# Block-sorted attention into a gated layer on one core: value products, a key-sort group and an exponential in another order within two down layers

## The chip, the cores and the metric

The kernel runs on one core of one Trainium2 chip. The metric is the device time of one execution in microseconds; lower is better. The inputs are 4 batches of 8 heads with 768 tokens of 64 values, and the weights of a gated layer of width 2048 on 512 features.

## The reference

Attention with sorted blocks, whose output goes through a gated layer. Per batch and head an 8x8 matrix `P` (five rounds of exponential and normalisation of `sort_net`) mixes the 8 blocks of 96 keys and of 96 values; each block of 96 queries attends to the mixed block in its place:

```python
k_sorted = np.einsum('bhij,bhjcd->bhicd', P, k_b).reshape(B, H, S, D)
v_sorted = np.einsum('bhij,bhjcd->bhicd', P, v_b).reshape(B, H, S, D)
...
scores = scale * np.matmul(q_b, k_sb.transpose(0, 1, 2, 4, 3))
scores = scores - np.max(scores, axis=-1, keepdims=True)
attn = np.exp(scores)
attn = attn / (np.sum(attn, axis=-1, keepdims=True) + 1e-09)
return np.matmul(attn, v_sb).reshape(B, H, S, D).astype(np.float32)
...
h = x @ w_in
g = h * np.cos(h)
return (g @ w_out).astype(np.float32)
```

## The kernel before

**Chunks and blocks.** The 3072 tokens are worked off in 8 chunks `n` of 384 tokens (half a batch), each of 4 blocks `u` of 96 queries. "Block (3,1)" is block 1 of chunk 3. A chunk goes through attention, then an up layer (`moe_up`) and a down layer (`moe_down`). The order of all instructions is written out by hand, engine by engine: each engine does its own in the order in which the code calls them. The attention of chunk n+1 (and the first scores of chunk n+2) stands between the matmuls of chunk n's layers.

**Attention of a block**, by name of the step:

- scores `sc`: 8 groups of matmuls of the block's queries (`q_turned`) on sorted keys (`kTs`), on TensorE (PE), by `by_half` (L504) or `scores` (L438);
- maximum `mx` (L489) and subtraction `s` (L491) on VectorE (DVE);
- `expo`: the exponential into `p_buf` on ScalarE (ACT, L570). Then `p_buf` is transposed into `pT`, by a DMA that SP issues (L588), or, with `True` as its last argument, later by PE (`p_transpose`). The `pT` of blocks (3,0) and (4,0) lies in a part of the buffer `kv`;
- `av`: the value product, 8 matmuls of 96x65 elements (L625) on sorted values `vS`; column 65 gives the sum. DVE normalises it into `xn` (L636, L638). `xn` is transposed into `xT` by a DMA of SP (L644), or, with `True`, by PE (`x_transpose`, L656, with a copy on DVE).

**Layers.** `up` is 8 matmuls of 384 columns into `h` (L669), a cosine on ACT (L673) and a product on DVE (L677); a chunk has 8 of them and they read all of its `xT`. `down(n, ts, half)` is 8 matmuls of 512 columns into `o` (L694) for 128 tokens; a chunk has three token tiles `ts` of two halves each. In `moe_down` these six are the steps e = 0 to 5: what stands in `slots[e]` comes behind step e, what stands in `mid[e]` between its fourth and fifth matmul. Behind a tile's second half its `o` is copied (ACT, or DVE for the last) and stored by SP (L684).

**Sorting.** The keys and values of the second pair of batches are sorted in groups: `k_sort_g` (4 matmuls `ks`, L408, and a cast on ACT into `kTs`, L257), and `batch`, which does several groups in a row: scores by `by_half`, keys (`ks`) or values (`vs`) by `sort_eight` (16 matmuls, L518, and a cast on ACT). When all keys are sorted, `k_swap(kT2)` moves two thirds of them to the other half of the partitions with two DMAs of SP (L421, L422); chunks 4 to 7 read the result.

**Buffers.** PSUM has 3 buffers of the pool `big` (scores, sort groups, value products, `h`) and 2 of `acc` (`o` and a few others). A tile takes the buffer that was given out longest ago and waits until its last reader is done.

**Queues.** SP issues, in this order, around the change: the transposes of chunk 3's queries (L149, two), of `pT` (2,0), (2,1), (2,2), two stores, `pT` (3,0), a store, the transposes of chunk 4's queries (L149, two), `k_swap` (L421, L422), `pT` (3,1), (3,2), a store, `pT` (3,3), `xT` (3,0), `xT` (3,1), a store. GpSimd (POOL) loads queries and values (L129, L92). Before chunk 4's queries it holds (`p_hold`, L596) until the `pT` of (2,2) has landed, and before chunk 5's until that of (3,3) has.

The change is in two places: chunk 1's down layer, written out at L1130 to L1154 of the kernel below, and the table of chunk 2's at L1162 to L1167.

Of the kernel before, what the change touches and what calls it, by code (L numbers as in the profile page):

```python
# [18 lines left out]
def kernel(  # L19
# [15 lines left out]
    nc = tc.nc  # L35
    B, H, S, D = q.shape
# [110 lines left out]
    def q_transpose_dma(n):  # L147
        for e in range(2):
            nc.sync.dma_start_transpose(  # L149
                out=q_of(n, e)[:, :QW].rearrange("p (x c) -> p x c", c=blk),  # L150
                in_=q_zeroed(n)[:, e * QZ:(e + 1) * QZ])
# [101 lines left out]
    V, A = nc.vector, nc.scalar  # L253

    def copy_on(eng, dst, src):
        if eng is nc.scalar:
            eng.copy(dst, src)  # L257
        else:
            eng.tensor_copy(dst, src)  # L259
# [147 lines left out]
    def k_products(ps, t, c, rows, rhs, keys=kbuf):  # L407
        nc.tensor.matmul(  # L408
            ps[:, t], keys[rows, c * 2 * D:(c + 1) * 2 * D], rhs, start=True, stop=True)

    def k_sort_g(t0, eng, pool, tag):
        ps = pool.tile([128, 4, 4 * NB], FP32, name="ks", tag=tag)
        for t in range(4):
            k_products(ps, t, t0 + t, slice(0, 128), bds[1].rearrange("p x i -> p (x i)"),
                       pair)
        copy_on(
            eng, kT2[:, ::2, :, :, t0:t0 + 4].rearrange("p e b m t -> p b e m t"),
            ps.rearrange("p t (b e m) -> p b e m t", b=2, e=2))
# [114 lines left out]
    def batch(*parts, between=()):  # L533

        tiles = []
        for kind, *x in parts:
            ps = big.tile([128, 2, 512], FP32, name=kind, tag="big")
            tiles.append(ps)
            if kind == "sc":
                by_half(*x, ps)  # L540
            else:
                sort_eight(kind, x[0], ps)
        step(between)
        for (kind, *x), ps in zip(parts, tiles):
            if kind == "sc":
                s_t[tuple(x)] = sp.tile([blk, 2, H2, blk], FP32, name="s", tag="s")
                qk_reduce(*x, [0, 1], ps)
            else:
                place_eight(kind, *x[:1], ps, x[1])
# [60 lines left out]
    def av(n, u, on_pe=False):  # L610
        av_products(n, u)
        av_norm(n, u, on_pe)

    def av_products(n, u, fill=0):
        g, b2, ih = where(n)
        if n not in xT:
            xT[n] = xtp.tile([128, KC, TC], BF16, name="xT", tag="xT")
        a = big.tile([128, 2, 512], FP32, name="av", tag="big")
        keep_warm(fill, a[:, 0], 256)
        pt = pT.pop((n, u)).rearrange("p a c -> p (a c)")  # L620
        for hp in range(2):
            for h2 in range(H2):
                e = hp * H2 + h2
                w = 128 if e < 2 * H2 - 1 else blk
                nc.tensor.matmul(  # L625
                    a[:w, hp, h2 * (D + 1):(h2 + 1) * (D + 1)],
                    pt[:blk, e * blk:e * blk + w],
                    vS[g][:, v_at(g, b2, hp, h2, ih * IC + u), :D + 1],
                    start=True, stop=True)
        av_ps[n, u] = a  # L630

    def av_norm(n, u, on_pe=False):
        avv = av_ps.pop((n, u))[:blk, :, :H2 * (D + 1)].rearrange(
            "p e (h w) -> p e h w", w=D + 1)
        r = small.tile([blk, 2, H2], FP32, name="r", tag="r")
        nc.vector.reciprocal(r[:].unsqueeze(3), avv[:, :, :, D:])  # L636
        xn = small.tile([blk, H2, 2, D], BF16, name="xn", tag="xn")
        nc.vector.tensor_tensor(  # L638
            xn.rearrange("p h e d -> p e h d"), avv[:, :, :, :D],
            r.to_broadcast([blk, 2, H2, D]), op=ALU.mult)  # L640
        if on_pe:
            xn_t[n, u] = xn
        else:
            nc.sync.dma_start_transpose(  # L644
                out=xT[n][:, :, u * blk:(u + 1) * blk],
                in_=xn.rearrange("p h e d -> p (h e d)"))
# [35 lines left out]
    def store(n, ts, o_s, eng=nc.sync):  # L682
        r0 = n * TC + ts * 128
        eng.dma_start(out=out[r0:r0 + 128, :], in_=o_s[:])  # L684
# [4 lines left out]
    def down(n, ts, half, stores, mid=(), late=()):  # L689
        if half == 0:  # L690
            out_ps[ts] = acc.tile([128, Dm], FP32, name="o", tag="acc")
        o = out_ps[ts]
        for f in range(half * FC // 2, (half + 1) * FC // 2):
            nc.tensor.matmul(  # L694
                o[:], gt[n, f // 4][:, f % 4, ts * 128:(ts + 1) * 128], w_out_t[:, f, :],
                start=(f == 0), stop=(f == FC - 1))
            if f % (FC // 2) == FC // 4 - 1:
                step(mid)
            if f % (FC // 2) == FC // 4:
                step(late)  # L700
        if half == 0:
            return
        if stores is None:

            z = (n % 2 * 3 + ts) * 2 * Dm
            o_s = vbuf[:, z:z + 2 * Dm].bitcast(FP32)
        else:
            o_s = op.tile([128, Dm], FP32, name="o_s", tag="o_s")
        late = n > 0 and ts == TC // 128 - 1
        copy_on(V if late else A, o_s[:], o[:])  # L710
        if stores is None or stores == "held":
            kept[n, ts] = o_s
        else:
            store(n, ts, o_s, nc.sync if late else stores)

    def step(calls):
        for f, *args in calls:
            f(*args)
# [6 lines left out]
    def moe_down(n, slots=(), stores=nc.sync, mid={}, late=()):  # L725

        for e in range(2 * TC // 128):
            last = e == 2 * TC // 128 - 1
            down(n, e // 2, e % 2, stores, mid.get(e, ()), late if last else ())
            step(slots[e] if e < len(slots) else ())  # L730

    B, C = (big, "big"), (acc, "acc")
# [400 lines left out]
    expo(2, 2)  # L1133
    let_go(1, 0)
    down(1, 1, 0, nc.sync)
    av(2, 0, True)
    down(1, 1, 1, nc.sync, mid=[(k_sort_g, 16, A, *B), (expo, 2, 3, True)])
    batch(("sc", 3, 0), ("ks", 1, A))
    p_hold(2, 2)
    for z in range(3, 6):  # L1140
# [19 lines left out]
    expo(3, 1)  # L1160
    expo(3, 2)
    moe_down(2, [[(ones, 1), (batch, ("sc", 3, 3), ("vs", 0, A))],  # L1162
                 [(batch, ("vs", 1, A)), (expo, 3, 3), (av, 3, 0)],
                 [(p_hold, 3, 3), (load_q, 5), (av, 3, 1),
                  (batch, ("vs", 2, A), ("sc", 4, 0))],
                 [(batch, ("vs", 3, A))], [(batch, ("vs", 4, A)), (expo, 4, 0), (sine_next,)]],
             mid={3: [(av, 3, 2, True)], 4: [(av, 3, 3, True)], 5: [(x_transpose, 3, 2, V, *B, 3)]})  # L1167
    q_transpose_dma(5)
    hold(q_turned[1])
    load_q(6)  # L1170
# [9 lines left out]
             None, mid={3: [(av, 4, 1)], 4: [(av, 4, 2, True)]},  # L1180
# [11 lines left out]
             None, mid={3: [(qk_av, 6, 1, 5, 2)]}, late=[(x_transpose, 5, 3, V, *B)])  # L1192
# [7 lines left out]
             None, mid={3: [(qk_av, 7, 1, 6, 2)]}, late=[(x_transpose, 6, 3, V, *B)])  # L1200
# [5 lines left out]
             mid={3: [(av, 7, 2)], 4: [(av, 7, 3, True)], 5: [(x_transpose, 7, 3, A, *B)]})  # L1206
# [45 lines left out]
```

## Time and profile before

| | |
|---|---|
| time, median of 3 runs | 234.93 us (234.88 to 235.5) |
| the profiled execution | 234.85 us, of which 233.1 us are the span from first to last instruction |
| granted TensorE clock | 1.00 |
| PE busy | 223.4 us (96%), 2268 matmuls |
| DVE busy | 170.9 us (73%) |
| ACT busy | 154.1 us (66%) |
| POOL busy | 96.0 us (41%) |
| chunk 1's down layer, chunk 2's up and down layer | from about 70, 86 and 98 us of the span; chunk 3's up layer from 114 us |

All times of the trace count from the start of the span. A row of the timeline has start, length, engine, line, operation, destination and source; in brackets stands the idle time before it and what ended it. A row of DMA issues ends with the microseconds from issue to landing. The page's share of the chain that ended last is 81% PE and 6% DMA.

### The profile page before, as it was taken

Reading aid. Unit: us, or ns where it says so; the run is one execution under the profiler, and the core shown is the slowest. Engines: PE = TensorE matmul, PEld = TensorE weight load, DVE = VectorE, ACT = ScalarE, POOL = GpSimd, SP = SyncE. Lnnn points to the kernel's source line nnn. Section 1 sums busy time; section 2 is a strip of 40 time slices with the busy share of each in tenths; the row PEclk is TensorE's granted clock in tenths of the full one; section 3 lists DMA queues with packets and bytes.
Section 4 is the critical chain, followed back from the end, with each engine's and each line's share of the span. In section 5 each row is a group of like instructions: output and inputs, shape, how many; then the busy total and the mean of one; then the engine's idle time right before and its main releaser. Section 6 shows DMA issues by size and latency. Waiting matters only on the chain.

```text
span 233.1 us, 5534 instructions
## 1 busy us (share of the span) xinstructions
PE 223.4 (96%) x2268; PEld 139.0 (60%) x2268; DVE 170.9 (73%) x291; ACT 154.1 (66%) x207; POOL 96.0 (41%) x121
## 2 busy tenths in 40 slices
PE   8789999999999799997999999999999999999994
PEld 3377898567664466644566456655665566556553
DVE  6769968969789577876398985997699769745700
ACT  5659877777889458795788665655665566816621
POOL 7999999399950287933617000900000000000000
PEclk9999999999999999999999999999999999999999
DMA  5999999994999699797999439973943450351012
GB/s 69 232 189 206 206 204 226 203 234 144 100 134 176 128 180 144 124 173 159 135 194 66 81 73 153 220 91 64 168 159 70 85 172 0 66 145 46 0 45 93
DMA packets 67673, 31.21 MB, mean 134 GB/s; under 512 B 56384, under 2 KB 63168, under 8 KB 67392
## 3 DMA queue, kind: packets, MB, share of 16 engines
q0 software_dynamic: 24048, 13.64, 44.2%
q1 hardware_dynamic: 43312, 17.02, 35.1%
q8 instruction: 18, 0.29, 0.5%
q10 hardware_dynamic: 288, 0.20, 0.3%
q14 instruction: 7, 0.06, 0.1%
HBM read 27.27 MB, written 6.29 MB: 144 GB/s over the span
## 4 chain that ended last, share of the span: by engine, by line
PE 81%; DMA 6%; DVE 5%; ACT 3%; POOL 2%; issue 1%; SPq 0%; ACTq 0%; POOLq 0%
PE h L669 30%; PE o L694 26%; PE h L857 5%; PE o L878 4%; DMA pT<-p_buf 4%; PE av L625 3%; PE sc L438 3%; PE ks L408 2%; DVE s L825 2%; DVE mx L821 2%; PE o L1216 2%; DMA kTs<-kTs 1%; PE xps L656 1%; ACT p_buf L570 1%; PE sc L504 1%
## 5 line engine op out<-in xcount | busy, mean ns | idle before, releaser
L669 PE MATMUL h<-xT,w_in_t 128*128 128x384 bf16 x448 | 78.4, 326 | 0.0
L694 PE MATMUL o<-w_out_t,gg 128*128 128x512 bf16 x320 | 76.2, 379 | 0.0
L677 DVE TENSOR_TENSOR gg<-c,h 128x768 bf16<-128x768 f32 x56 | 52.7, 949 | 19.6 <-ACT c L673 19.6
L673 ACT ACTIVATE c<-h,half_pi 128x768 f32<-128x768 f32 x56 | 50.5, 901 | 24.9 <-PE h L669 24.0
L669 PEld LDWEIGHTS <-w_in_t 128*128 128x128 bf16 x448 | 42.3, 98 | 26.3 <-issue 0.5
L694 PEld LDWEIGHTS <-gg 128*128 128x128 bf16 x320 | 28.9, 99 | 28.4
L179 POOL COPY vperm<-kv 64x768 bf16<-64x768 bf16 (+2 forms) x12 | 28.4, 2412 | 4.3 <-DMA kv<-in_v_dram 4.3
L570 ACT ACTIVATE p_buf<-s 96x768 bf16<-96x768 f32 x32 | 26.6, 842 | 5.3 <-DVE s L491 4.0
L491 DVE TENSOR_TENSOR s<-sc,mx 96x384 f32<-96x384 f32 (+1 forms) x33 | 24.3, 736 | 1.6
L489 DVE TENSOR_REDUCE mx<-sc 96x4 f32<-96x384 f32 (+1 forms) x33 | 24.0, 728 | 1.3 <-PE sc L504 1.3
L638 DVE TENSOR_TENSOR xn<-av,r 96x512 bf16<-96x512 f32 x32 | 22.0, 687 | 1.1
L129 POOL DMA_DIRECT2D kv<-in_q_dram x24 | 16.0, 681 | 0.8 <-issue 0.8
L257 ACT CAST kTs<-ks 128x512 bf16<-128x512 f32 (+1 forms) x18 | 11.0, 631 | 7.6 <-PE ks L408 6.7
L257 ACT COPY kv<-o 128x512 f32<-128x512 f32 (+2 forms) x10 | 5.2, 524 | 14.1 <-PE o L694 11.5
L636 DVE RECIPROCAL r<-av 96x8 f32<-96x8 f32 x32 | 6.4, 199 | 10.8 <-PE av L625 10.3
L129 POOL DMA_DIRECT2D q_mem<-in_q_dram x16 | 10.7, 691 | 2.6 <-DMA kv<-in_v_dram 2.3
L878 PE MATMUL o<-w_out_t,gg 128*128 128x512 bf16 x48 | 11.7, 379 | 0.0
L438 PE MATMUL sc<-kTs,q_turned 128*128 128x96 bf16 x152 | 11.0, 206 | 0.2 <-DMA kTs<-kTs 0.2
L259 DVE COPY kv<-o 128x512 f32<-128x512 f32 (+1 forms) x5 | 3.1, 611 | 11.1 <-PE o L1216 8.5
L857 PE MATMUL h<-xT,w_in_t 128*128 128x192 bf16 x128 | 11.1, 246 | 0.0
L596 POOL CAST held<-q_turned 96x1 f32<-96x1 bf16 x2 | 0.4, 183 | 25.3 <-DMA q_turned<-q_mem 18.8
L257 ACT CAST pair<-vs 96x512 bf16<-96x512 f32 (+1 forms) x11 | 8.6, 780 | 3.0 <-PE vs L518 3.0
(134 smaller groups left out, 288.8 us busy)
## 6 DMA issues: line engine op xcount, KB each, us to landing
out_dram<-kv SPq DMA_DIRECT2D x12, 256.0 KB, 2.6
out_dram<-o_s SPq DMA_DIRECT2D x10, 256.0 KB, 3.4
w_in_t<-in_moe_w_in_dram POOLq DMA_DIRECT2D x4, 512.0 KB, 11.5
w_out_t<-in_moe_w_out_dram POOLq DMA_DIRECT2D x4, 512.0 KB, 12.2
kv<-in_k_dram POOLq DMA_DIRECT2D x2, 768.0 KB, 10.1
kv<-in_v_dram POOLq DMA_DIRECT2D x2, 768.0 KB, 13.2
pair<-in_k_dram POOLq DMA_DIRECT2D x2, 768.0 KB, 12.4
kv<-in_v_dram POOLq DMA_DIRECT2D x6, 256.0 KB, 6.2
```

The lines of the kernel that those rows point to most:

```text
L129: nc.gpsimd.dma_start(out=q_heads[:, i, :, e], in_=src[:, ih * IC + i, :, e])
L179: nc.gpsimd.tensor_copy(dst, src)
L257: eng.copy(dst, src)
L489: nc.vector.reduce_max(mx[:], scv, axis=AX.X)
L491: nc.vector.tensor_tensor(s, scv, mx.to_broadcast(list(s.shape)), op=ALU.subtract)
L570: nc.scalar.activation(p[:, :, :blk], s_t.pop((n, u)).rearrange("p e h c -> p (e h) c"), AF.Exp, scale=scale)
L638: nc.vector.tensor_tensor(xn.rearrange("p h e d -> p e h d"), avv[:, :, :, :D], r.to_broadcast([blk, 2, H2, D]), op=ALU.mult)
L669: nc.tensor.matmul(h[:, f2, :w], w_in_t[:, kk, f * 128:(f + 1) * 128], xT[n][:, kk], start=(kk == 0), stop=(kk == KC - 1))
L673: nc.scalar.activation(c[:], h[:, :, :w], AF.Sin, bias=half_pi[:, 0:1])
L677: nc.vector.tensor_tensor(gt[n, fp // 2][:, f:f + 2], c[:], h[:, :, :w], op=ALU.mult)
L694: nc.tensor.matmul(o[:], gt[n, f // 4][:, f % 4, ts * 128:(ts + 1) * 128], w_out_t[:, f, :], start=(f == 0), stop=(f == FC - 1))
L857: nc.tensor.matmul(o[:, part, f2 * w:(f2 + 1) * w], w_in_t[:, kk, f * 128:(f + 1) * 128], xT[0][:, kk, h * w:(h + 1) * w], start=(kk == 0) ...
```

## The change

No instruction is added or removed. In chunk 1's down layer the key-sort group with keys 16 to 19 moves from the middle of the second half of token tile 1 to its start, and the value product of block (2,0) from the start to the middle. In chunk 2's down layer the exponential of (3,3) goes ahead of the value sort group 1; the value product of (3,1) moves from slot 2, where it stood ahead of a value sort group and the scores of (4,0), into the middle of step 3; and the product of (3,2) moves from the middle of step 3 to behind value sort group 3 in slot 3.

```diff
     down(1, 1, 0, nc.sync)
-    av(2, 0, True)
-    down(1, 1, 1, nc.sync, mid=[(k_sort_g, 16, A, *B), (expo, 2, 3, True)])
+    k_sort_g(16, A, *B)
+    down(1, 1, 1, nc.sync, mid=[(av, 2, 0, True), (expo, 2, 3, True)])
...
     moe_down(2, [[(ones, 1), (batch, ("sc", 3, 3), ("vs", 0, A))],
-                 [(batch, ("vs", 1, A)), (expo, 3, 3), (av, 3, 0)],
-                 [(p_hold, 3, 3), (load_q, 5), (av, 3, 1),
-                  (batch, ("vs", 2, A), ("sc", 4, 0))],
-                 [(batch, ("vs", 3, A))], [(batch, ("vs", 4, A)), (expo, 4, 0), (sine_next,)]],
-             mid={3: [(av, 3, 2, True)], 4: [(av, 3, 3, True)], 5: [(x_transpose, 3, 2, V, *B, 3)]})
+                 [(expo, 3, 3), (batch, ("vs", 1, A)), (av, 3, 0)],
+                 [(p_hold, 3, 3), (load_q, 5), (batch, ("vs", 2, A), ("sc", 4, 0))],
+                 [(batch, ("vs", 3, A)), (av, 3, 2, True)], [(batch, ("vs", 4, A)), (expo, 4, 0), (sine_next,)]],
+             mid={3: [(av, 3, 1)], 4: [(av, 3, 3, True)], 5: [(x_transpose, 3, 2, V, *B, 3)]})
```

How the instructions stand on PE in chunk 1's down layer, at the border between the two halves of token tile 1 (`pT_1510` is the transposed probability of (2,0), `pair` the keys to sort; DMAHW0 is the semaphore of that transpose). Before:

```order
L694 MATMUL o_1582<-w_out_t_97,gg_1370 128x512
L625 LDWEIGHTS pT_1510 [waits DMAHW0_49]
L625 MATMUL av_1592<-vS_110,pT_1510 128x65 [waits Activation_49]
...
L694 LDWEIGHTS gg_1423
...
L408 LDWEIGHTS pair_89
L408 MATMUL ks_1609<-bd1_152,pair_89 128x128 [waits DVE_49]
...
L694 LDWEIGHTS gg_1477
```

And in the changed kernel:

```order
L694 MATMUL o_1582<-w_out_t_97,gg_1370 128x512
L408 LDWEIGHTS pair_89
L408 MATMUL ks_1591<-bd1_152,pair_89 128x128 [waits Activation_49]
...
L694 LDWEIGHTS gg_1423
...
L625 LDWEIGHTS pT_1510 [waits DMAHW0_49]
L625 MATMUL av_1602<-vS_110,pT_1510 128x65 [waits DVE_49]
...
L694 LDWEIGHTS gg_1477
```

The product that waits for the DMA has changed places with the 4 `ks` matmuls; the 4 `o` matmuls on `gg_1423` stay between them.

On PE in chunk 2's down layer, behind the first half of token tile 1 (`pT_1947` is that of (3,1), `q_turned0` chunk 4's queries; DMAHW1 and DMAHW2 are the semaphores of the two swaps, DMAHW7 and DMAHW0 those of the query transposes, DMAHW3 that of `pT_1947`). Before:

```order
L694 MATMUL o_2040<-w_out_t_97,gg_1831 128x512
L625 LDWEIGHTS pT_1947 [waits DMAHW3_49]
...
L518 LDWEIGHTS vperm_88 [waits Pool_49]
...
L504 LDWEIGHTS q_turned0_94 [waits DMAHW1_49,DVE_49,DMAHW7_49]
L504 MATMUL sc_2089<-kTs_98,q_turned0_94 128x96 [waits PE_49]
L504 LDWEIGHTS q_turned0_94 [waits DMAHW0_49]
L504 MATMUL sc_2089<-kTs_98,q_turned0_94 128x96 [waits DMAHW2_49]
...
L694 LDWEIGHTS gg_1876
```

And in the changed kernel:

```order
L694 MATMUL o_2040<-w_out_t_97,gg_1831 128x512
L518 LDWEIGHTS vperm_88 [waits Pool_49]
...
L504 LDWEIGHTS q_turned0_94 [waits DMAHW1_49,DVE_49,DMAHW7_49]
L504 MATMUL sc_2075<-kTs_98,q_turned0_94 128x96 [waits PE_49]
L504 LDWEIGHTS q_turned0_94 [waits DMAHW0_49]
L504 MATMUL sc_2075<-kTs_98,q_turned0_94 128x96 [waits DMAHW2_49]
...
L694 LDWEIGHTS gg_1876
...
L625 LDWEIGHTS pT_1947 [waits DMAHW3_49]
```

The product of (3,1) with its wait has moved behind the scores of (4,0), whose second pair of weights and matmul waits for the second query transpose and the second swap.

On DVE in the same place (`r` and `xn` are the normalisation of a product, `mx` and `s` the maximum and subtraction of the scores of (4,0)):

```order
-L636 RECIPROCAL r<-av 96x8
-L638 TENSOR_TENSOR xn<-av,r 96x2x4x64
-L489 TENSOR_REDUCE mx<-sc 96x8
-L491 TENSOR_TENSOR s<-sc,mx 96x768
+L489 TENSOR_REDUCE mx<-sc 96x8
+L491 TENSOR_TENSOR s<-sc,mx 96x768
+L636 RECIPROCAL r<-av 96x8
+L638 TENSOR_TENSOR xn<-av,r 96x2x4x64
```

The normalisation of (3,1) now stands behind the scores' two instructions. The orders of SP and POOL are the same in both kernels.

## The prediction

> **What bounds the kernel now.** I read the list of what each engine waited for first, then the busy time by stage, then the chain of work that ended last around the two places that the change touches. TensorE (PE) carries the kernel. In the list of waits of PE, one entry is larger than all others:
>
> ```profile
> PE av L625 <- DMA pT<-p_buf: 2.4, 2, 1.2
> ```
>
> Twice, for 1.2 us each, a value product (`av`) waits until SP's DMA has transposed its probabilities (`pT`). The busy time by stage (chunk 1's down layer, chunk 2's up layer, chunk 2's down layer, chunk 3's up layer) says where, and that nothing else is lost there:
>
> ```profile
> 70.00:86.00 16.00, 14.81 (x172) 8.11 (x170) 12.43 (x22) 11.26 (x15) 5.80 (x10) 1.00 1.00 161
> 86.00:98.00 12.00, 12.00 (x103) 7.87 (x102) 9.22 (x14) 9.78 (x14) 10.01 (x6) 1.00 1.12 131
> 98.00:114.00 16.00, 14.83 (x187) 7.77 (x186) 10.47 (x17) 11.24 (x14) 8.16 (x11) 1.00 1.04 167
> 114.00:127.00 13.00, 13.00 (x114) 8.57 (x113) 10.00 (x14) 10.79 (x16) 6.05 (x10) 1.00 1.31 130
> ```
>
> The second and third columns are the stretch and PE's busy time: 16.00 - 14.81 = 1.19 us idle in chunk 1's down layer, 1.17 us in chunk 2's, none between and none behind, at a granted clock of 1.00. So PE is the bound, the two waits are all that another order could win here, about 2.36 us, and work that PE does earlier shortens the run by as much, unless it meets a date that something else sets.
>
> **Chunk 1: the key-sort group first.** The chain there (start, length, what):
>
> ```profile
> 73.04 4.13 DMA pT<-p_buf
> 77.22 0.43 PE av L625 x8
> 77.65 0.87 PE o L694 x4
> 78.52 0.22 PE ks L408 x4
> 78.74 0.86 PE o L694 x4
> 79.60 0.28 PE sc L504 x8
> ```
>
> `pT` of block (2,0) lands at 73.04 + 4.13 = 77.17; PE ran dry at 77.22 - 1.19 = 76.03. The change adds no work: the same 4 `ks` (0.22 us) and 4 `o` (0.87 us) stand ahead of the product instead of behind it. 0.22 + 0.87 = 1.09 us go into the hole of 1.19, and about 0.1 us of wait is left. The transfer was issued at 73.04, long before, by a queue whose order is unchanged, so I leave 77.17 where it is. Behind the product there is then one `o` group instead of two and the `ks`: the next scores start at 77.65 + 0.87 = 78.52 instead of 79.60. **Saved: 1.08 us.**
>
> What must be ready earlier for that? The moved `ks` takes a PSUM buffer that ACT or DVE leaves before 76, and the product one of an earlier score:
>
> ```profile
> 73.66 0.99 ACT L257 CAST kTs<-ks 128x1024 bf16<-128x1024 f32 x1
> 75.70 0.95 DVE L491 TENSOR_TENSOR s<-sc,mx 96x768 f32<-96x768 f32 x1
> 74.37 2.19 SPq L588 DMA_TRANSPOSE pT<-p_buf  x1
> pT<-p_buf SPq DMA_TRANSPOSE x1, 4.1
> ```
>
> These end at 74.65 and 76.65. The next product, of block (2,1), moves from 80.11 to 79.03; its `pT` was issued at 74.37 and lands 4.1 us later, at 78.47: 0.5 us to spare. The exponential of (2,3) waits on ACT behind the cast of the moved `ks`; both come earlier. I cost these edits at nothing; the thinnest cover is that 0.5 us. DVE and ACT follow PE here, and chunk 2's up layer has no hole, so the 1.08 us reaches chunk 2's down layer whole.
>
> **Chunk 2: the product of (3,1) behind the scores of chunk 4.** The chain of before:
>
> ```profile
> 101.59 4.54 DMA pT<-p_buf
> 106.18 0.43 PE av L625 x8
> 106.61 0.36 PE vs L518 x16
> 106.97 0.17 PE sc L504 x8
> 107.14 0.97 PE o L694 x4
> 108.10 0.26 PE av L625 x8
> 108.36 0.86 PE o L694 x4
> 109.23 0.36 PE vs L518 x16
> 109.58 0.97 PE o L694 x4
> ```
>
> PE is dry from 106.18 - 1.17 = 105.01, and 1.08 us earlier after the change: 103.93. Then it runs `vs` (0.36 us) to 104.29 and comes to the scores of (4,0), which used to stand behind the wait. They need chunk 4's swapped keys, and those have a date of their own:
>
> ```profile
> 94.03 3.62 SPq L149 DMA_TRANSPOSE q_turned<-q_mem  x2
> 97.74 1.12 SPq L421 DMA_DIRECT2D kTs<-kTs  x1
> 98.91 0.59 SPq L422 DMA_DIRECT2D kTs<-kTs  x1
> kTs<-kTs SPq DMA_DIRECT2D x1, 384.0 KB, 4.5
> kTs<-kTs SPq DMA_DIRECT2D x1, 384.0 KB, 6.5
> SPq L149 <- DMA q_mem<-in_q_dram: 6.7, 1, 6.7
> 79.65 0.18 POOL L596 CAST held<-pT 96x1 f32<-96x1 bf16 x1 [12.54 <-DMA pT<-p_buf]
> ```
>
> The second swap (L422) is issued at 98.91 and lands 6.5 us later, at 105.41. It does not come earlier with PE: it stands on SP behind the two transposes that start at 94.03, and these wait 6.7 us for query loads that POOL starts only after the hold at 79.65, which waits for the `pT` of (2,2), a transfer issued before the change touches anything. So from the second weights on the scores start at 105.41 + 0.05 = 105.46 (0.05 us also lie between 106.13 and the product at 106.18): a wait of 105.46 - 104.29 = 1.17 us, as long as the old one and under another name. **The transfer that was hidden behind the late `pT` is what is late next.** The 8 score matmuls then take 0.17 to 0.28 us (both are in the chains above), and the first `o` starts at about 105.70 instead of 107.14. From there: `o` 0.97, to 106.67, where `pT` of (3,1) has been there since 101.59 + 4.54 = 106.13; the product 0.26, to 106.93; `o` 0.86, to 107.79; `vs` 0.36, to 108.15; the product of (3,2), which the change puts here, 0.26, to 108.41; and the next token tile's `o`, which began at 109.58. That is 1.17 us earlier; with the longer scores 1.1. **In all the kernel is 1.1 us earlier behind this place, not 1.08 + 1.17**: what chunk 1 gave is waited away, and chunk 2's order wins it again.
>
> The landing of L422 is the disputed price. From below: the first swap's 4.5 us, 103.41, no wait at all. From above: the 7.7 us that a transpose of this queue took under other loads (quoted with the slower rival), 106.61, which leaves 1.1 - 1.2 = -0.1 us. I take 6.5 us, since it is this transfer in this place, and keep both ends.
>
> A rule speaks for the lower end. The Trainium skill, "DMA: Bandwidth & Descriptors", section "Anatomy of one DMA", gives a DMA about 2.0 us fixed plus its bytes at 436 GB/s. By it the second swap would land, as an estimate from that page, at 98.91 + 2.0 + 0.9 = 101.8 and the sum would be a saving of 2.2 us. The row says 6.5 us, so the trace does not agree here, where the queue is full.
>
> The other moves. ACT does the exponential of (3,3) one cast earlier; its transpose comes earlier to a queue that is busy, and the POOL hold behind it cannot get later by that: nothing. DVE now normalises (3,1) behind the scores' maximum and subtraction:
>
> ```profile
> 107.49 0.94 DVE L489 TENSOR_REDUCE mx<-sc 96x8 f32<-96x768 f32 x1
> 109.64 0.69 DVE L638 TENSOR_TENSOR xn<-av,r 96x512 bf16<-96x512 f32 x1
> xT<-xn SPq DMA_TRANSPOSE x1, 2.3
> 109.06 2.66 POOL L129 DMA_DIRECT2D kv<-in_q_dram  x4 [0.29 <-issue]
> 113.83 1.29 PEld L669 LDWEIGHTS <-w_in_t 128*128 128x128 bf16 x8
> ```
>
> The first two rows are the maximum of these scores and the end of the next normalisation, with the subtraction and a reciprocal between: 109.64 + 0.69 - 107.49 = 2.84 us. The change has the same four instructions in the same order, from about 105.8 to 108.7. Then SP issues the transpose of that block's `xn`; 2.3 us later (the same transfer's landing before), at 111.0, it is there. Chunk 3's up layer needs it at 113.83 - 1.1 = 112.7. There are 1.7 us to spare, but it now goes out close to POOL's query loads, which start at 109.06.
>
> The sum, against the profiled execution: 234.85 - 1.1 = 233.75 us. The median of the runs, 234.93, lies 0.08 above that execution, so I forecast **233.8 us**, 0.5% faster. A measurement of this kernel can tell about 0.3%, 0.7 us, from no change.
>
> **Rivals.** *Both waits go* (20%). The first swap needed 4.5 us, and something in this stretch moves with PE:
>
> ```profile
> q8 instruction: 1, 0.02, 5.5%
> ```
>
> That is the DMA activity from 103.0 to 104.4: one load of 0.02 MB of instructions, in the middle of the two landings that PE waits for. When PE is earlier, the load is, and the queue may drain sooner. Against it: each DMA engine still has the same bytes to move. (The Trainium skill, "Runtime: NRT & Kernel Launch", section "Instruction fetch mechanics", calls such loads of 16 KiB mostly hidden; by that, moving it changes nothing, and no run here shows its price yet.) If the swap lands by 104.3 and the `pT` of (3,1) still at 106.13, the product starts at 106.18 and the `o` behind it at 106.44 instead of 108.36, less 0.26 for the product of (3,2): 1.66 saved, 233.3 us. If both land early, 1.08 + 1.17 = 2.25 saved: 232.7 us.
>
> *The swap lands later* (15%): the product of (3,1) is no longer a filler, and each 0.1 us of landing costs 0.1. At 7.0 us of landing 0.6 is saved, at 7.7 nothing: 234.3 to 235.0 us.
>
> *Slower* (12%): the transpose of `xn` of (3,1), issued at 108.7, falls among POOL's query loads. Two transposes of before did, those of (4,0) and (3,0):
>
> ```profile
> 113.85 1.21 SPq L588 DMA_TRANSPOSE kv<-p_buf  x1
> kv<-p_buf SPq DMA_TRANSPOSE x1, 5.2
> kv<-p_buf SPq DMA_TRANSPOSE x1, 7.7
> ```
>
> 5.2 and 7.7 us instead of 2.3. With 5.2 it lands at 113.9, and chunk 3 starts 0.1 us later than before; with 7.7 at 116.4, 2.6 us later. It begins to cost at 4.0 us of landing, where 112.7 is passed, and decides from 5.8 us on, where the run is slower by over 0.3%: 235.6 to 237.5 us. Against it: POOL's loads start with a hold that waits for the same queue, and the first of these two was issued 4.8 us into such a run of loads, not ahead of one.
>
> **How the numbers follow.** Forecast 53%, both waits go 20%, later swap 15%, slower 12%. The predicted time is the forecast's. The range leaves out the slower case and the last of the later swap, and reaches down to 232.7 with 0.1 for the measurement: 232.6 to 234.8. Faster by over 0.3% (under 234.2): the forecast and both waits going, 0.73. Within 0.3%: the later swap, 0.15. Slower: 0.12.
>
> **What would show it.** In the changed profile the product of (2,0) waits 0.1 us at 77.2 and the scores behind it start at 78.5. In chunk 2 the product of (3,1) waits for nothing, and the weights of the scores of (4,0) wait about 1.2 us for the swap of `kTs`, landing at 105.4. Chunk 3's up layer starts at 112.7, without a wait for `xT`, and PE has no new hole behind it. I am wrong if the swap lands at another time, if `pT` of (2,0) does not land at 77.17, or if chunk 3's first weights wait for `xT`.

## The result, and the profile after

The changed kernel takes 233.38 us (median of 9 runs, 232.86 to 234.27), the kernel before 234.93 (9 runs, 234.06 to 235.5). The ratio is 0.9941 with a 95% interval of 0.992 to 0.9962: 0.6% faster, and the interval does not touch 1. A ratio here is that of the means of the runs that lie within 1.5% of a kernel's fastest, so it need not be the quotient of the medians. Forecast were 233.8 us and 1.1 us of saving; measured is 1.55 between the medians and 234.85 - 233.38 = 1.47 between the two profiled executions. The new span is 231.6 us.

First the list of what PE waited for, in the stages that the change touches. Over chunk 1's down layer (70 to 86 us) it is empty. Over chunk 2's (98 to 114) it has one entry:

```profile
PE sc L504 <- DMA kTs<-kTs: 0.5, 1, 0.5
```

No product (`av`) waits for `pT` any more. The wait has moved to the scores of (4,0) and the swapped keys, under the name that the prediction gave it, but at 0.5 us and not 1.2. The busy time by stage, with the same columns as before:

```profile
70.00:86.00 16.00, 16.00 (x181) 8.95 (x180) 13.52 (x24) 12.42 (x16) 5.79 (x10) 1.00 0.94 159
...
98.00:114.00 16.00, 15.55 (x194) 8.11 (x192) 10.35 (x18) 12.21 (x15) 7.76 (x11) 1.00 1.04 160
114.00:127.00 13.00, 13.00 (x113) 8.33 (x111) 10.75 (x16) 10.91 (x15) 5.45 (x10) 1.00 1.00 122
```

PE's hole of 1.19 us in chunk 1 is gone, that of 1.17 us in chunk 2 is 16.00 - 15.55 = 0.45 us, and chunk 3's up layer still has none. Together 1.19 + 0.72 = 1.91 us; this execution came to chunk 1's down layer 0.39 us later than the one before it did, on PE's timeline (the first `o` group behind the second scores at 72.80 instead of 72.41), ahead of everything that the change touches, and 1.91 - 0.39 = 1.52 is what is seen behind: chunk 3's up layer starts at 112.56 instead of 114.04. The chain through chunk 2's down layer (start, length, what):

```profile
98.13 6.82 DMA kTs<-kTs
104.94 0.04 issue
104.98 0.33 PE sc L504 x7
105.31 0.97 PE o L694 x4
106.28 0.26 PE av L625 x8
106.54 0.86 PE o L694 x4
107.40 0.36 PE vs L518 x16
107.76 0.36 PE av L625 x8
108.12 0.86 PE o L694 x4
```

The order behind the swap is that of the prediction's list, piece by piece. The swap is again slow, 6.8 us, but it was issued at 98.13 instead of 98.91.

### The profile page after: what moved, and what is told of

It is laid out like the page before. It is cut to its first block, busy times and chain, and to the rows that moved or that the text cites. A ratio compares the mean times of both kernels' runs of the same rounds, so it can differ in the third digit from the quotient of the medians.

```text
span 231.6 us, 5534 instructions
## 1 busy us (share of the span) xinstructions
PE 223.5 (97%) x2268; PEld 138.9 (60%) x2268; DVE 170.9 (74%) x291; ACT 154.2 (67%) x207; POOL 95.9 (41%) x121
## 4 chain that ended last, share of the span: by engine, by line
PE 85%; DMA 5%; DVE 3%; POOL 2%; ACT 2%; issue 1%; SPq 1%; POOLq 0%; ACTq 0%
PE h L669 30%; PE o L694 28%; PE h L857 5%; PE o L878 5%; DMA kTs<-kTs 4%; PE av L625 3%; PE sc L438 3%; PE ks L408 2%; PE o L1215 2%; PE pps L835 1%; PE xps L656 1%; PE sc L504 1%; PE vs L782 1%; PE xps L844 1%; SPq L421 1%
## 5 line engine op out<-in xcount | busy, mean ns | idle before, releaser
L669 PE MATMUL h<-xT,w_in_t 128*128 128x384 bf16 x448 | 78.4, 326 | 0.0
L669 PEld LDWEIGHTS <-w_in_t 128*128 128x128 bf16 x448 | 42.2, 98 | 26.5 <-DMA xT<-xn 0.4
L438 PEld LDWEIGHTS <-q_turned 128*128 128x128 bf16 x152 | 8.8, 98 | 3.0 <-issue 0.6
L857 PEld LDWEIGHTS <-w_in_t 128*128 128x128 bf16 x128 | 10.5, 98 | 0.0
```

Source lines behind the costliest of these rows:

```text
L438: nc.tensor.matmul(out, q_of(n, hp)[:, x:x + 128], keys_of(n, u, h2, hp), start=True, stop=True)
L669: nc.tensor.matmul(h[:, f2, :w], w_in_t[:, kk, f * 128:(f + 1) * 128], xT[n][:, kk], start=(kk == 0), stop=(kk == KC - 1))
L857: nc.tensor.matmul(o[:, part, f2 * w:(f2 + 1) * w], w_in_t[:, kk, f * 128:(f + 1) * 128], xT[0][:, kk, h * w:(h + 1) * w], start=(kk == 0) ...
```

## Experiments

**Theory of the prediction, fixed dates (T1 here).** PE meets dates that other engines set; the second swap's date does not move with PE, so each part alone saves 1.1 us at most and both together no more. **Rival (T2).** The change moves the date too, by what it does to SP and POOL earlier. A second question is why the swap and the transpose land so late at all: the queue ahead of them, or the load of instructions in between.

### Each part alone: c1_only, c1_again, c2_only

c1_only is the kernel before with chunk 1's lines alone, and c1_again the same kernel once more; c2_only has the table of chunk 2 alone.

```diff
 c1_only, c1_again
-    av(2, 0, True)
-    down(1, 1, 1, nc.sync, mid=[(k_sort_g, 16, A, *B), (expo, 2, 3, True)])
+    k_sort_g(16, A, *B)
+    down(1, 1, 1, nc.sync, mid=[(av, 2, 0, True), (expo, 2, 3, True)])
 c2_only
     the moe_down(2, ...) call of the changed kernel, the two lines above as before
```

> Only chunk 1's two lines are changed. Theory of dates (what the product of (3,1) waits for is set by SP's queue and not by PE): PE reaches chunk 2's wait 1.1 us earlier and waits about that much longer for the pT of (3,1); the product's wait grows from 1.2 to about 2 us and the time stays within 0.5 us of before, 234.4 to 234.9 us. Rival (the queue moves with PE, so gains add up): 1.1 us saved, 233.8 us, and the wait stays at 1.2 us.

> Chunk 1's two lines alone, a second time, since its first profile had the product of (3,1) waiting 1.3 us while the swap came 1.2 us earlier than before. If the dates follow chunk 1's order (through the store that then finds the DMA engines idle), the loads again take 13.5 us from POOL's hold to the query transposes, the wait is again 1.3 us and 0.6 to 1.1 us are saved, 233.8 us. If that was chance, the loads take 14.0 to 14.4 us as in the two kernels without this edit, and at most 0.4 us is saved.

> Only chunk 2's table is changed; chunk 1 keeps its wait of 1.2 us. Theory of dates: PE comes to the scores of (4,0) at about 105.4 of its span, just when the second swap lands, so they wait 0.1 us at most and the product of (3,1) not at all: 1.1 us saved, 233.8 us. Rival (one wait is only exchanged for another of the same length): nothing saved, 234.9 us.

Measured: c1_only 234.13 us against 234.68, ratio 0.9991 (0.9964 to 1.0017), which does not tell it from no change; c1_again 233.93 against 234.84, 0.997 (0.9948 to 0.9991), faster; c2_only 233.78 against 234.68, 0.9958 (0.9941 to 0.9975). The waits of PE from 98 to 114 us in c1_again:

```profile
PE av L625 <- DMA pT<-p_buf: 1.7, 1, 1.7
```

In c1_only that wait was 1.3 us. So chunk 1's 1.08 us are only partly waited away again: by a fixed date the wait would have grown from 1.17 to 2.25. It grew by 0.1 and by 0.5, since the `pT` of (3,1) landed at 104.97 and 105.39, 1.2 and 0.7 us earlier than the 106.13 of before. T1 gets this step wrong. c2_only, in which chunk 1 is as before, behaves by T1: the swap was issued at 98.84 and took 6.6 us, so that its date stayed at 105.4. PE comes there 1.1 us later than with both parts, and in chunk 2 it waits for nothing (idle 16.00 - 15.84 = 0.16 us). In time the interval of c2_only overlaps that of the whole change, so what chunk 1's order adds to it is read from the profiles.

### What moves the date: late_store and after_again

The SP queue of the kernel before, ahead of the swaps:

```profile
77.95 3.05 SPq L684 DMA_DIRECT2D out_dram<-o_s  x2
83.01 1.31 SPq L588 DMA_TRANSPOSE kv<-p_buf  x1
86.76 0.33 SPq L684 DMA_DIRECT2D out_dram<-o_s  x1
```

and of the changed kernel:

```profile
78.13 1.59 SPq L684 DMA_DIRECT2D out_dram<-o_s  x2
81.97 1.45 SPq L588 DMA_TRANSPOSE kv<-p_buf  x1
85.90 0.33 SPq L684 DMA_DIRECT2D out_dram<-o_s  x1
93.28 3.59 SPq L149 DMA_TRANSPOSE q_turned<-q_mem  x2
96.97 1.11 SPq L421 DMA_DIRECT2D kTs<-kTs  x1
98.13 0.59 SPq L422 DMA_DIRECT2D kTs<-kTs  x1
```

The two stores of each first row belong to token tiles 0 and 1. Before, they end at 77.95 + 3.05 = 81.00, after at 78.13 + 1.59 = 79.72, since the second waits for its tile and the tile is ready earlier. POOL's loads for chunk 4 start behind the hold, at 79.65 before, and after at

```profile
79.84 0.18 POOL L596 CAST held<-pT 96x1 f32<-96x1 bf16 x1 [13.09 <-DMA pT<-p_buf]
```

So the 256 KB of the second store now go out 1.3 us earlier, ahead of those loads. POOL's waits of before, from 78 to 100 us:

```profile
POOL q_mem L129 <- DMA kv<-in_v_dram: 2.3, 2, 1.3
```

and of the changed kernel:

```profile
POOL q_mem L129 <- DMA kv<-in_v_dram: 1.5, 2, 0.8
```

The last query loads wait 0.8 us less for the value loads ahead of them, and from the hold to the first query transpose on SP it is 93.28 - 79.84 = 13.44 us instead of 94.03 - 79.65 = 14.38. late_store tests it: the changed kernel with that one store held back, behind the exponential of (3,0) and its transpose.

```diff
-    down(1, 1, 1, nc.sync, mid=[(av, 2, 0, True), (expo, 2, 3, True)])
+    down(1, 1, 1, "held", mid=[(av, 2, 0, True), (expo, 2, 3, True)])
...
     expo(3, 0)
+    let_go(1, 1)
```

> The changed kernel, with the store of chunk 1's token tile 1 issued behind the transpose of the pT of (3,0) instead of ahead of it, which is about 4 us later and within POOL's loads, as it fell before the change. Theory of the free DMA time (with the change that store runs while the DMA engines are idle, so POOL's loads, the query transposes and the swap behind them come 0.9 us earlier): the loads take about 14.2 us again from the hold to the query transposes instead of 13.4, the swap lands 0.5 to 0.8 us later, the scores of (4,0) wait about 1.1 us instead of 0.5, and the time is about 234.0 us, 0.6 above the changed kernel. Rival (the earlier swap was chance, or follows PE for another reason): the loads take 13.4 us as in the changed kernel and the time is the changed kernel's, 233.4 us.

> The changed kernel once more, unchanged, for a second profile beside the one with the late store. Theory of the free DMA time: 13.4 us again from POOL's hold to the query transposes, the swap lands at 104.7 to 105.0, the scores of (4,0) wait 0.4 to 0.8 us, 233.4 us. Rival (that swap was early by chance): 14.0 us or more, and a wait of about 1.1 us as with the late store.

Measured: late_store 233.92 us against 234.84, ratio 0.9966 (0.9948 to 0.9983); the changed kernel once more, after_again, 233.51 against 234.58, 0.9949 (0.9926 to 0.9972). SP of late_store:

```profile
81.66 1.59 SPq L588 DMA_TRANSPOSE kv<-p_buf  x1
83.30 2.61 SPq L684 DMA_DIRECT2D out_dram<-o_s  x2
94.20 3.64 SPq L149 DMA_TRANSPOSE q_turned<-q_mem  x2
97.94 1.14 SPq L421 DMA_DIRECT2D kTs<-kTs  x1
99.13 0.59 SPq L422 DMA_DIRECT2D kTs<-kTs  x1
```

Its waits, on POOL in the loads and on PE in chunk 2's down layer:

```profile
POOL q_mem L129 <- DMA kv<-in_v_dram: 2.3, 1, 2.3
...
PE sc L504 <- DMA kTs<-kTs: 1.1, 1, 1.1
```

With the hold at 79.61, that is 14.59 us to the first transpose, POOL's 2.3 us are back, and so is the wait that the prediction named, 1.1 us of 1.17. The two repeats agree by the same row: 1.3 to 1.5 us of this POOL wait and 13.25 to 13.5 us where chunk 1 has the new order (after_again, c1_only, c1_again), 2.5 and 13.99 in c2_only, which has the old one. In after_again the swap was issued at 97.79 and landed at 104.35, just as PE came to it, and the stage has no wait at all. The third value load separates the two cases without an overlap: it landed 6.3 to 6.6 us after its issue where the store is ahead of the loads (the changed kernel, after_again, c1_only, c1_again, and f_before and f_after below, the first of which has the old order), and 7.2 to 7.5 where the store is beside them (the kernel before, c2_only, late_store). **T2 is shown** by the rows: chunk 1's order sends a store out ahead of POOL's loads, and the date moves by 0.5 to 1.1 us against the kernel before. Against late_store, where the swap was issued at 99.13 and landed at 105.25, it is 0.3 and 0.9 us. In time, late_store lies 0.4 to 0.5 us over the two medians of the changed kernel; their intervals overlap, so the size rests on the profiles.

### Queries first: q_first, q_before, q_first_hold

If POOL's loads set the date, chunk 4's query loads ahead of the value loads should remove the wait. q_first does this to the changed kernel, q_before to the kernel before. q_first_hold adds to q_first that chunk 5's query loads wait until `xT` of (3,1) has landed.

```diff
 q_first, q_before, q_first_hold
     p_hold(2, 2)
+    load_q(4)
     for z in range(3, 6):
         load_pair(vbuf, vin_d, z * CD // 6, (z + 1) * CD // 6)
-    load_q(4)
 q_first_hold, besides
+    def x_hold(n, u):
+        nc.gpsimd.tensor_copy(held[:], xT[n][:, 0, u * blk:u * blk + 1])
...
-                 [(p_hold, 3, 3), (load_q, 5), (batch, ("vs", 2, A), ("sc", 4, 0))],
-                 [(batch, ("vs", 3, A)), (av, 3, 2, True)], ...
+                 [(batch, ("vs", 2, A), ("sc", 4, 0))],
+                 [(x_hold, 3, 1), (load_q, 5), (batch, ("vs", 3, A)), (av, 3, 2, True)], ...
```

> The changed kernel, and POOL issues chunk 4's query loads ahead of the three value loads instead of behind them. Theory of dates: the query transposes and the swap behind them come some 2 us earlier or more, the scores of (4,0) no longer wait for the swap (0.45 us of wait go), and PE has no hole in chunk 2's down layer: 0.4 to 0.6 us below the changed kernel, about 232.9 us. Rival (the swap is late for its own bytes and not for its start): the wait stays. What could go wrong is the value loads: if they are too late for the permutation, a value sort group waits and the time rises.

> The kernel before, with chunk 4's query loads ahead of the three value loads and nothing else changed. Theory of dates: the swap and the pT of (3,1) behind it land early (about 101.3 and 104.3), the product of (3,1) waits 0.2 us at most instead of 1.2, the product of (2,0) still waits 1.2 us: 1.0 to 1.2 us saved, 233.7 us. Rival (the pT of (3,1) is late for its own transfer and the instruction load alone): its wait stays above 0.8 us, and at most 0.3 us is saved.

> The kernel with chunk 4's query loads ahead of the values, and chunk 5's query loads held until the transpose of xn of (3,1) has landed instead of the pT of (3,3). Theory (that transpose takes 4.3 us instead of 2.3 because it falls among these loads and then ends PE's wait ahead of chunk 3's up layer): it lands in 2.4 us, chunk 3's first weights do not wait, and 0.1 to 0.3 us are saved over the kernel with the loads first, 232.5 us. Rival (it is late for the instruction load near 109 us): it still takes 4 us, and nothing is saved.

Measured: q_first 232.71 us against 234.68, ratio 0.9914 (0.9893 to 0.9935): the lowest median of all, 0.7 to 0.8 us below the changed kernel's, though the intervals of the two just overlap. q_before 233.69 against 234.58, 0.9961 (0.9948 to 0.9975). q_first_hold 233.03 against 234.84, 0.9933 (0.9908 to 0.9957). SP of q_first:

```profile
86.78 8.14 SPq L149 DMA_TRANSPOSE q_turned<-q_mem  x2
95.59 0.47 SPq L421 DMA_DIRECT2D kTs<-kTs  x1
96.11 0.59 SPq L422 DMA_DIRECT2D kTs<-kTs  x1
100.26 3.12 SPq L588 DMA_TRANSPOSE pT<-p_buf  x2
```

The query transposes go out 6.5 us earlier than after the change, take 8.1 us of SP instead of 3.6 (now they run beside the value loads), and the swap is still issued 2.0 us earlier. No `sc` or `av` of this stage waits; what is left there is next in line:

```profile
PE h L669 <- DMA xT<-xn: 0.3, 1, 0.3
```

In q_before, which has neither part of the change, the product of (3,1) no longer waits at all and the stage is idle for 0.32 us; only chunk 1's wait is left, and that was 0.7 us instead of 1.19:

```profile
PE av L625 <- DMA pT<-p_buf: 0.7, 1, 0.7
```

So the wait of chunk 2 could be removed without the new order. But it was not the expected earlier date: that `pT` was issued at 101.94, 0.35 us later than in the kernel before, and took 2.9 us instead of 4.5; the next experiment bears on why. q_first_hold misses its aim: with the loads held until 111.66 the transpose of `xn` of (3,1) takes 3.9 instead of 4.7 us, where the theory had 2.4 and the rival, PE's load of instructions, 4. Chunk 3's up layer does start at 111.32 instead of 111.88, without a wait. But chunk 5's loads now start 4.1 us later than in q_first (107.60) and chunk 6's 2.1 us later (123.62 against 121.49). A `pT` that q_first issues behind these, at 127.66, is issued among them here, at 127.09, and takes 4.6 us instead of 2.8, so that in chunk 3's down layer a product waits for it (line 628 is line 625 here):

```profile
PE av L628 <- DMA pT<-p_buf: 0.7, 1, 0.7
```

Chunk 4's up layer starts at 137.39 against 137.30 in q_first. What was gained is given back 20 us later, and the time, 0.3 us over q_first's with overlapping intervals, shows no gain.

### Why the landings are slow: f_before, f_after, qf_mid, qf_early

In the middle of the two slow landings PE fetches 16 KB of instructions, one of 18 such fetches for its 4536 matmuls and weight loads. These kernels move that fetch and leave the rest in its order: the warm-up matmuls at the start, which compute nothing that is used, get another number, so that the fetches fall elsewhere.

```diff
-    keep_warm(14, big.tile([128, 512], FP32, name="idle", tag="big"))
+    first = big.tile([128, 512], FP32, name="idle", tag="big")
+    keep_warm(4, first)
+    for _ in range(116):
+        nc.tensor.matmul(
+            first[:32, :32], warm[:, :32], warm[:, :1].to_broadcast([128, 32]),
+            start=True, stop=True)
```

That is f_before and f_after (of the kernel before and the changed one). qf_mid and qf_early do it to q_first, with 13 long and 19 short, and with 12 long and 42 short.

> The kernel before with other warm-up matmuls at the very start: 4 of 512 columns and 116 of 32 instead of 14 of 512, which is 212 PE instructions more. Nothing else is changed. Every load of PE instructions (one per 256) then falls 212 instructions earlier, or 44 later than another load fell. Theory of the instruction load (the two pT land late because such a load holds up one DMA engine at 74.5 and 103.1): the loads are now about 2 us later, both pT land about 1 us earlier, both waits of 1.2 us shrink below 0.4, and about 2 us are saved: 233 us. Rival (the queue is simply full): the waits stay and the time is that of before, 234.9 us.

> The changed kernel with the other warm-up matmuls (212 PE instructions more at the start), one look for the landings. Theory of the instruction load: with no load of instructions between the swap and the pT of (3,1), the second swap lands 5.2 us after its issue and that pT 2.9 us after its own, as in the kernel before with this warm-up, and the scores of (4,0) wait 0.2 us at most. Rival: 6.8 and 4.9 us as in the changed kernel.

> This is q_first with one of the 14 long warm-up matmuls at the start replaced by 19 short ones, so that PE's later loads of instructions (one per 256 of its instructions) fall 36 instructions earlier, about 1.5 us by the 24 per us of this stage: the load of 100.2 goes to about 98.7, into the middle of the second swap's transfer (issued 96.1, landed 101.27 in q_first). Theory L (a load of instructions on one DMA engine holds up whatever transfer is in flight there): the swap lands 1.2 to 1.6 us later after its issue, 6.4 to 6.8 us instead of 5.2, and the transpose of (3,1) stays at 2.9. Theory Q (the swap is long only where the queue ahead of it is full, and loads do not matter): 5.2 and 2.9 us as in q_first. Neither costs time, since the swap then lands by 102.8, before its scores: 232.4 to 233.4 us by both.

> As qf_mid, with two warm-up matmuls replaced by 42 short ones: 80 instructions more, so that the load falls about 3.3 us earlier than in q_first, at 96.9, just behind the second swap's issue and during the first swap (issued 95.6, landed 99.35 in q_first, 3.8 us). Theory L: the first swap takes 4.9 to 5.4 us instead of 3.8 and the second 5.2 to 6.8, by how far the delay is carried on. Theory Q: 3.8 and 5.2 us. Both expect 232.4 to 233.4 us, and a wait for the swap by neither.

Measured: f_before 236.86 us against 234.68, ratio 1.0019 (0.9998 to 1.0039): six of its twelve runs lie at 234.4 to 235.7 us, on which the ratio rests, and six at 238.0 to 240.1, for a reason that no trace here shows. The 2 us that were expected to be saved are not seen in the time. f_after, one run, 233.21; qf_mid and qf_early, one run each, 234.19 and 233.66 beside 234.14 of the kernel before. f_before comes to chunk 1's down layer 1.5 us later than the kernel before (71.39 against 69.90), and qf_mid and qf_early have waits of 1.1 us for `xT` and 0.6 us for a transposed probability in the last 40 us that q_first has not, so the totals say nothing on the fetch; the landings and waits do. Both waits of the kernel before shrink in f_before, about as expected: the one of chunk 1 is gone, that of chunk 2 is 0.4 us. In f_before the swap and the `pT` of (3,1) were issued within 0.25 us of where the kernel before issued them, and the fetch fell at 104.6, behind both. SP's issues in f_before:

```profile
97.48 1.15 SPq L425 DMA_DIRECT2D kTs<-kTs  x1
98.68 0.60 SPq L426 DMA_DIRECT2D kTs<-kTs  x1
101.72 2.57 SPq L592 DMA_TRANSPOSE pT<-p_buf  x2
```

then the landing of that `pT`, which took 4.5 us before:

```profile
pT<-p_buf SPq DMA_TRANSPOSE x1, 2.8
```

and the swap's in f_after, which took 6.8 us after the change:

```profile
kTs<-kTs SPq DMA_DIRECT2D x1, 384.0 KB, 5.1
```

The swap of f_before took 5.2 us and the `pT` of f_after 2.9. So both landings are shorter by 1.4 to 2.0 us where the fetch is moved, and in f_after PE loses 16.00 - 15.83 = 0.17 us in the stage. That speaks for the fetch, though in f_after it fell at 103.5, still within the flight of that `pT`.

For the transposes the traces settle it. The same edit moved the fetch of 74.5 us to 78.4 in f_before and to 77.9 in f_after. With it, the `pT` of (2,0), issued at 73 to 74.5 us, fell from 4.1 and 4.0 us to 2.8 in both, and that of (2,2), issued behind it at about 77, rose from 2.9 to 4.0. The rows for (2,2) in the kernel before, then in f_before:

```profile
pT<-p_buf SPq DMA_TRANSPOSE x1, 2.9
pT<-p_buf SPq DMA_TRANSPOSE x1, 4.0
```

Four transposes, the `pT` of (2,0), (2,2) and (3,1) and the `xn` of (3,1), in all 14 traces give 56 landings. In 27 of them the fetch starts 0.8 to 2.2 us behind the issue, and they took 3.6 to 5.5 us. In the other 29 it starts elsewhere, in some just at the issue, and they took 2.3 to 2.95. Only at the edge, 2.2 us behind, do both occur. In q_first, q_before and q_first_hold the fetch starts within 0.04 us of the issue of the `pT` of (3,1), which takes 2.9 us; by these rows that is enough to explain its short landing there.

For the swap it is not settled. qf_early speaks against the simple form: there the fetch fell at 97.1, into the middle of both swaps,

```profile
q8 instruction: 1, 0.02, 5.8%
...
kTs<-kTs SPq DMA_DIRECT2D x1, 384.0 KB, 4.3
```

and the first swap took 4.3 us instead of q_first's 3.8, the second 5.2 as in q_first. A fetch there costs one swap 0.5 us and the other nothing. qf_mid missed its aim: the fetch went to 100.85, not 98.7, in the swap's last microsecond as in q_first (100.24), and the landings were q_first's, 5.2 and 2.9 us. So **for the swap neither "a fetch holds up whatever is in flight" nor "only the full queue counts" fits all rows**: with the queries last, all runs with the fetch in its old place have 6.1 to 6.8 us and the two with it moved have 5.1 and 5.2; with the queries first it is 5.2 wherever the fetch falls. Moving it also moved the fetch before (90.4 in the kernel before, 92.9 in f_before), so for the swap the cause may lie in either, and stays open.

## Why the prediction was right, and where it was off

- **PE is the bound and the two waits are all there is: right.** 1.91 us of holes went, and 1.48 us of start of chunk 3's up layer came out of it, less 0.39 that this execution was late beforehand.
- **Chunk 1 saves 1.08: right.** The `pT` of (2,0) landed at 77.39 in this run, not 77.17, for it was issued 0.37 us later, and the product started at 77.44 on PE's timeline, without a wait; the scores behind it start at 78.67, forecast 78.5. Nothing moved into the hole waits for anything.
- **The wait goes over to the second swap: right in kind.** It is the row of the first fence above.
- **"It does not come earlier with PE": wrong, and this is the term that was mis-sized.** The forecast date was 105.41, the measured 104.94 and, in the second profile, 104.35. The prediction followed the queue back to POOL's hold and stopped there, at a date that is indeed fixed (79.65 and 79.84); it did not ask what else uses the DMA engines between the hold and the loads' end. The store of token tile 1 does, and it comes from the work that chunk 1's order moves. late_store shows it: 14.59 us instead of 13.44, and the wait back. The forecast of 1.1 us would have been right for that kernel: 0.9 us measured between its medians.
- **Landing of 6.5 us: nearly right, 6.8.** The rival by which both waits go (20%) was the other half of the truth in its date, the swap landing by 104.3, which is the second profile. It was not so in its reason, a queue that drains sooner: the swap took 6.8 and 6.6 us, no less than before, and was issued earlier. The time lies between forecast and rival. The rule that the prediction set against its own row, from the Trainium skill, "DMA: Bandwidth & Descriptors", section "Anatomy of one DMA", would have had the swap land 2.9 us after its issue by its figures, as an estimate. The section gives these figures for DMAs that GpSimd issues, and the swap is issued by SP; no run shows 2.9 us, the shortest second swap took 5.1.
- **The rival that the swap lands later (15%): did not come.** Its landing was 0.3 us longer, its issue 0.8 us earlier.
- **The slower rival (12%): the long landing came, at no price, and mostly for another cause than the rival gave.** The transpose of `xn` of (3,1) went out at 108.22 and took 4.3 us:

```profile
xT<-xn SPq DMA_TRANSPOSE x1, 4.3
...
PEld L669 <- DMA xT<-xn: 0.4, 1, 0.4
```

It landed at 112.51 and PE's first matmul of chunk 3 started at 112.56. It is past the 4.0 us from which it was to cost, and met PE to within 0.05 us, which was luck; the 0.4 us are the weight load's, which runs beside PE. In q_first, where PE is earlier, it does cost 0.3 us. The forecast 2.3 us of landing was wrong, and the 1.7 us to spare were used up. The rival put the length down to POOL's query loads. In f_after, the changed kernel with the fetch moved from 110.45 to 112.34, behind the landing, the transpose took 2.9 us, though the loads start only 0.43 us behind it. In q_first_hold, with the loads held back and the fetch 1.7 us behind the issue, it took

```profile
xT<-xn SPq DMA_TRANSPOSE x1, 3.9
```

By these two runs PE's fetch is the larger part and the loads the smaller. The prediction said that the fetches come earlier with PE, but looked for the effect at the swap alone.
- **Signs of being wrong.** The prediction named three and all came: the swap at another time, the `pT` of (2,0) 0.22 us past 77.17, and a wait of chunk 3's first weights. The time was in the range even so, since the swap was only 0.5 us off and the others cost nothing.

## What to carry to other kernels

When a wait is filled, follow the next one back through every queue to the date that sets it, and then ask which transfers share the DMA engines with those loads: a store that leaves 1.3 us earlier, ahead of a burst of loads and not in it, moved the date of a transfer 20 us later by 0.5 to 1.1 us. Where the order of work and the order of loads both lead to the same wait, try the loads first: one moved call (q_before) took as much as the new order of chunk 2, and the change with that call moved as well (q_first) is faster than either. A hold that protects one transfer (q_first_hold) can be paid for by one behind it. And before the queue or the loads are blamed for a late transpose, look whether an instruction fetch falls into its flight: work that moves on PE moves the fetches too.

## What the runs showed of the hardware

- Where one store goes decides what it and the loads behind it take. The second store of chunk 1, 256 KB, landed 4.5 us after its issue in the kernel before, 2.0 us in the changed one, where it is 1.3 us earlier and the DMA engines had little else, and in late_store, amid POOL's loads, after

```profile
out_dram<-o_s SPq DMA_DIRECT2D x1, 256.0 KB, 8.6
```

- A fetch of 16 KB by PE lengthens a DMA transpose in flight. The `pT` of (3,1) took 4.2 to 5.5 us in the seven runs where the fetch starts 1.2 to 2.2 us behind its issue, and 2.8 to 2.95 in the seven others. Six of the seven long ones landed 2.8 to 3.0 us behind the start of the fetch, the one of late_store 3.8. Moving the fetch was worth 1.2 to 2.0 us on the transposes that it left. The prediction cited the Trainium skill, "Runtime: NRT & Kernel Launch", section "Instruction fetch mechanics", for such fetches being mostly hidden; the price seen here falls on transfers of another queue. On the swaps qf_early shows 0.5 us on one and none on the other, and these runs do not settle what a fetch costs there.
- Loads add to a transpose's landing as well, by less here. POOL's query loads start at 109.06 before, 0.8 us behind the issue of the `xn` transpose of (3,1), and after at

```profile
108.84 2.66 POOL L129 DMA_DIRECT2D kv<-in_q_dram  x4 [0.29 <-DMA xT<-xn]
```

With no fetch in its flight it took 2.3 us before and 2.9 in f_after, where the loads start 0.43 us behind it; with a fetch, 3.9 with the loads held back (q_first_hold) and 4.7 with them (q_first). In the other runs with both it took 3.9 to 4.3, so the size of this part is uncertain.
